# Cluster products and the sums and mean of w_out issued in halves, with a new order of work up to the first h

## The chip, the cores and the metric

The kernel runs on one core of a Trainium2 chip. One launch does the whole computation. The metric is the device time of that launch in microseconds (us); the median of three runs of the kernel before is 223.88 us, the lowest 223.83 and the highest 224.02. The profiles are of single executions, taken by the hardware profiler; each has a time of its own.

The core has engines that run beside each other, each with its own list of instructions that it works through in order: PE (the matrix engine; its weight loads are listed apart as PEld), DVE (VectorE), ACT (ScalarE), POOL (GpSimd) and SP (SyncE, which here only issues transfers). They wait for each other by semaphores.

## The reference

Two layers, cut to what matters. The first is attention in which a query sees only the keys of its own cluster:

```
q, k, v: (4, 8, 768, 64); centroids: (8, 16, 64)
q_assign = argmax(einsum('bhsd,hcd->bhsc', q_n, c_n))      # q_n, k_n, c_n: rows of length 1
k_assign = argmax(einsum('bhsd,hcd->bhsc', k_n, c_n))
mask     = q_assign[:, :, :, None] == k_assign[:, :, None, :]
scores   = where(mask, q @ k^T / sqrt(64), -1e9)
x        = softmax(scores) @ v                             # then laid out as (3072, 512)
```

The second works on each of the 3072 rows (tokens):

```
h    = x @ w_in                          # w_in (512, 1024)
solu = h * softmax(h)
ln   = (solu - mean(solu)) / sqrt(var(solu) + 1e-6) * g_ln
out  = ln @ w_out                        # w_out (1024, 512)
```

Since the mean that is taken from `solu` is the same number for all 1024 columns of a row, the kernel takes it out of `w_out` instead: it multiplies `w_out` by `g_ln`, subtracts from every row the mean over the 1024 rows, and multiplies `solu` by the result. For that it needs, once, the sums of `g_ln * w_out` over the rows, and their mean.

## The kernel before

The work is cut into named operations. A helper class, `Weave`, collects them (`add`, line 104) with the operations that each needs, and then issues them in an order that is written out by hand: `ORDER` (lines 28 to 78) has for each engine a list of kinds with counts ("S3" is the next three operations of kind S on that engine). What must wait for what on the chip comes from the data that the operations read and write, not from these lists; the lists only say what stands behind what on each engine.

The kinds that matter here:

- `ld`, `lv`, `li`, `lo` on SP: loads of q and k, of v, of w_in (four pieces `li0` to `li3`) and of w_out (four pieces `lo0` to `lo3`).
- `tp` on PE and `xa` on DVE or ACT (batch 0), `xt` on DVE (batches 1 to 3): q and k of a pair of heads transposed into a tile `xt`, one for q and one for k. `ca`: their cast into `qk`, from which the scores are made.
- `cl` on PE (`clusters`, line 445): the products of a pair's q and k with its centroids, into a tile `csc`. It is four float32 matmuls of 32 output rows and 384 columns, each in its own quarter (32 columns) of the PE array, two for q and two for k. The trace has two records for each float32 matmul.
- `tb`, `mx`, `oh`, `ot` on DVE: transpose, maximum, one-hot and transpose back (tile `oht`, in batch 0 a part of `w_out_c`); `pl`, mostly on POOL: the one-hots put under the rows of `qk`; `bl`: a part of them cleared. After that the scores of the pair can be made. One-hots on both sides add a constant to the scores of equal clusters, which serves as the mask.
- `S` on PE (`scores`): one bank of scores of 512 columns, mostly two matmuls of 256 columns; `E` on ACT (`expo`): its exponential; `V` on PE (`values`): the product with v for 128 queries, six matmuls. The scores have three banks (`ps_s`), so the bank of `S` number i is free when `E` number i-3 is done. `N` on DVE: division by the sums.
- `tx` on SP: x transposed by a transfer. `h` on PE (`f_h`): x times w_in for a block of 128 tokens, in four quarters of two matmuls each; `hm`, `ex`, `u`: maximum (DVE), exponential (ACT) and product (DVE); `tu`: u transposed by a transfer; `y` on PE (`f_y`): times w_out.
- `gs` on POOL, `su` on PE (`sum_w_out`, line 579), `sk` on DVE, `me` on PE (`mean_w_out`, line 592), `ce` on DVE: the mean taken out of w_out. `su0` and `su1` are four float32 matmuls each, of 32 output rows and 512 columns, again each in its own quarter of the PE array. `me` is one float32 matmul of 128 rows and 512 columns.
- `wi0` to `wi3` on POOL (line 561): the four quarters of w_in cast to bfloat16.

The four matmuls of one `cl`, in batch 0:

```python
for c in range(4):
    i, hh = divmod(c, 2)
    nc.tensor.matmul(csc[c * NB:(c + 1) * NB, :n], c_by_two[:, 2 * p + hh],
                     xts[b, p, i][:, hh * HALF:(hh + 1) * HALF],
                     tile_position=(0, c * NB))
```

Sixteen pairs of heads (four batches of four) go through `cl`, the first of them in two halves of the tokens. Batch 0 is worked off first in the order of the scores; the second layer begins, with the first `h`, about a fifth into the time, and from there scores, values, `h` and `y` of different blocks alternate on PE.

Of the kernel before, what the change touches and what calls it, by code (L numbers as in the profile page):

```python
# [10 lines left out]
F32 = mybir.dt.float32  # L11
# [11 lines left out]
class Weave:  # L23
# [3 lines left out]

    ORDER = {}
    ORDER["SP"] = """
        ld4 si ld4 lg lv ld2 lv ld3 lo ld lv ld2 lv ld2 lo2 ld3 lo ld4 li ld li3 tx ld lv  # L30
        ld3 lv tx ld3 tu ld8 lv tu tx ld lv ld4 tu ld3 ou ld2 ou ld tu ld12 tu ld4 lv ld2 ou
        tx ld3 tu ou ld2 tx lv ld tu ld4 tx ld tu ou2 ld lv ld4 tu ld4 tu ld ou ld7 pl ou ld
        lv2 ld3 tu lv tx ou tu lv pl ld4 ou2 tx lv tu tx ou tu pl2 tu2 tx tu tx ou2 tx ou tu
        tx2 ou tu2 ou2 tu2 ou6
    """
    ORDER["POOL"] = """
        po zo ca3 z ca pl ca bl pl2 ca bl ca pl sg cv z ca3 cv ca pl cv pl2 ca gs pl2 ca pl
        z ca2 cv2 z2 ca2 pl2 cv pl wi ca2 wi pl wi pl wi pl bl cv pl ca pl at pl cv al ca cv
        pl at ca bl pl cv ca3 al at ca al ca at ca pl2 bl cv pl2 ca4 at ca2 al ca pl2 bl pl2
# [5 lines left out]
        fl wm fl tp2 cp fl2 cl tp fl tp fl4 cl S3 tp2 S2 tp2 cq S2 tp S tp S2 tp S cl S2 V S  # L45
        tp S V S V S gt V S V2 S cl S V S V S V S tp S tp S2 tp S V S tp V2 S2 cl S3 V2 S V
        S V S2 V S V2 S2 V S cl S3 V2 S V S V S su S3 V2 S V S V S su S3 V2 S V2 S2 me S3 V2
        S V S V S cl S2 V S V S V2 S2 h S h S2 h2 S V2 S2 h V2 S h S V2 S2 h S V S V S h S h
        S2 V S h V S y2 V2 S2 y V S V S h3 S3 y V3 h V S2 V2 S cl S3 h2 S2 V3 S y2 S V h2 S
        V y2 S h S V h S2 h S y3 S2 y V3 h S3 cl V2 S V S y S2 y2 S3 V3 S y S2 V3 S2 cl S V  # L50
        S2 V2 S h S2 V2 S V S h S2 V2 cl V2 S3 y2 S V S2 V y S2 y V2 S3 h2 S V h S h S2 V h
        S V S V y2 S h V y2 S2 V S h3 S cl V S2 V2 S h V cl S3 h2 V y V S3 y2 V S h V3 S y S
        h S2 h2 S3 V2 y h S V S2 y V3 y S3 h3 y S3 V3 S h S V S V cl S V S h S cl V2 S3 y V2
        S y S2 y V2 S3 h y V S3 V h V2 S3 cl S2 V2 S y3 S2 y S V3 S V S y S2 V S V3 S2 y2 S3
        y V2 S2 h V2 S3 h3 S V S2 V y S V h2 V2 S y S2 y V y S h2 S3 cl h V S2 V3 S h V2 S3
        h2 S y S2 V h S2 V y2 V4 S3 y h S2 h V h V S V S y2 S3 V3 h2 S2 h2 S2 y2 S V S h2 S
        V3 S2 h S h S2 V S y V2 S V y2 S2 h2 S2 h2 V2 S2 V2 y S2 h V2 h V S2 h S V h S3 V2 h
        y S V y3 V h3 S2 y3 S2 y h2 V2 h y h y3 h V h V y4 h ptx h y4 h2 y3 h2 y ptu2 y6 ptu
        y ptu y5
    """  # L60
    ORDER["DVE"] = """
        cn xa cb ca tb mx oh ot pl2 tb mx oh ot xa3 cf xa2 ca cv tb xa mx oh gk N ot pl tb
        xa mx xa oh xa ot N tb mx pl N xt2 cv N oh ot N pl tb mx N oh ot sk xt N xt ce3 N ce
        tb ce ca ce2 N ce hm mx N u oh bn2 N hm ot ag xt u xt N bn2 hm ag sc xt u N bn tb hm
        mx bn oh ag u xt bn ot xt N cv hm bn ag sc xt tb mx N u xt oh ot sc N bn2 xt ag xt
        tb N hm mx tb N oh ot u xt mx N bn oh bn xt hm ot ag N cv u bn2 xt hm tb mx u N tb
        oh mx hm ot bn2 oh ag u N sc ag hm bn ot u bn N xt2 ag xt2 hm tb N bl mx tb bn2 oh u
        N xt ag xt sc hm ot tb mx oh N bn sc N u bn N ag xt ot bn ca N mx sc oh hm u bn ag N
        xt hm bn2 bl tb u ot ag N hm mx bn2 u bn N oh ot hm bl2 u ag N cv hm sc bn u N hm ag
        bn N bn u bn2 hm ag2 N bn u bn2 N ag hm bn u N ag hm bn2 u bn2 hm sc u N ag2 bn tx  # L70
        hm bn sc u bn ag hm bn tu ag u2 bn2 ag sc
# [104 lines left out]
def kernel(  # L176
# [185 lines left out]
    def apart(b, p):  # L362


        return by_token(b) and not halves_of(b, p)
# [76 lines left out]
            VEC[e].tensor_scalar(dst, src, scalar1=inv_C, scalar2=1.0,  # L442
                                 op0=Alu.mult, op1=Alu.mult)

    def clusters(b, p, hf):

        lo, n = (0, HALF) if hf is None else (hf * HALF, QTR)
        csc = ps_m.tile([P, HALF], F32, name="csc", tag="m")
        if apart(b, p):
            for c in range(4):  # L450
                i, hh = divmod(c, 2)
                nc.tensor.matmul(csc[c * NB:(c + 1) * NB, :n], c_by_two[:, 2 * p + hh],  # L452
                                 xts[b, p, i][:, hh * HALF:(hh + 1) * HALF],
                                 tile_position=(0, c * NB))
        for c in range(4) if not apart(b, p) else ():
            i, part = divmod(c, 2)
            nc.tensor.matmul(csc[c * NB:(c + 1) * NB, :n], c_bd[:, p, :],  # L457
                             xts[b, p, i][:, lo + part * n:lo + (part + 1) * n],
                             tile_position=(0, c * NB))
        asg[b, p, hf, "csc"] = csc  # L460
        asg[b, p, hf, "n"] = n

    def turn_back(b, p, hf):
        n = asg[b, p, hf, "n"]
# [111 lines left out]
    def spread_g():  # L576
        nc.gpsimd.tensor_copy(g_cols, g_ln2[:].unsqueeze(2).to_broadcast([P, n_fc, NB]))

    def sum_w_out(r):

        for c in range(4):
            fc = 4 * r + c
            uses(nc.tensor.matmul(hreg[c * NB:(c + 1) * NB, 1, :], g_cols[:, fc, :], w_g[:, fc, :],  # L583
                                  start=(r == 0), stop=(r == n_fc // 4 - 1),
                                  tile_position=(0, c * NB)), 1)
# [3 lines left out]
        uses(nc.scalar.copy(w_sum[:], src) if e == "ACT" else  # L589
             nc.vector.tensor_copy(w_sum[:], src), 1)  # L590

    def mean_w_out():
        uses(nc.tensor.matmul(hreg[:, 2, :], g_mean[:], w_sum[:]), 1, 2)  # L593

    def centre_w_out(fc):
        uses(nc.vector.scalar_tensor_tensor(out=w_out_c[:, fc, :], in0=w_g[:, fc, :],
# [393 lines left out]
    for idx, (b, p) in enumerate(pairs):  # L990
        first = first_of(b, p)
        for hf in range(2) if halves_of(b, p) else (None,):
# [6 lines left out]
            add(f"cl{t}", "PE", (0.72 - 0.22 * hf if half else 0.87), first - 9,  # L999
                (lambda e, b=b, p=p, hf=hf: clusters(b, p, hf)), kept + ["cf" if apart(b, p) else "cb"], take="m")  # L1000
# [116 lines left out]
    for f in range(n_f):  # L1117
# [113 lines left out]
    add("gs", "POOL", 0.35, 20, lambda e: spread_g(),  # L1231
        ["gk", "wm"] + [f"fl{j}" for j in range(n_idle)])
    for r in range(n_fc // 4):
        add(f"su{r}", "PE", 1.06, 30 + r, (lambda e, r=r: sum_w_out(r)),
            ["gs", f"lo{2 * r}", f"lo{2 * r + 1}"] + ring_free(1),
            last_tp[-1:] + [f"su{x}" for x in range(r)])
    add("sk", "DVE", 0.6, 34, keep_sums, [f"su{n_fc // 4 - 1}"], also={"ACT": 0.48})
    add("me", "PE", 0.9, 36, lambda e: mean_w_out(), ["sk", "sg"] + ring_free(2), last_tp[-1:])
    for fc in range(n_fc):
        add(f"ce{fc}", "DVE", 0.66, 44 + 0.5 * fc, (lambda e, fc=fc: centre_w_out(fc)),  # L1240
            ["me"] + [f"{x}0.{p}" for x in ("cl", "ot") for p in range(1, n_pair)],
            [f"ce{fc - 1}"] if fc else [])

    def clear(z):
# [35 lines left out]
```

## Time and profile before

| | |
|---|---|
| median of three runs | 223.88 us |
| the profiled execution, its time | 223.47 us |
| its span, first to last instruction | 221.6 us |
| PE busy | 215.8 us (97%) |
| DVE busy | 196.1 us (89%) |
| ACT busy | 191.8 us (87%) |
| POOL busy | 129.5 us (58%) |
| first `h` starts | 44.86 us |

The profiled execution's time is 1.87 us more than its span, and 0.41 us less than the median. A busy PE is not a PE at its peak: the ends of matmuls are modelled, and a matmul that waits in the array's queue counts as busy; so waits on PE are read from the distance between the starts of its pieces of work, not from its busy time. The granted clock of PE is 1.00 throughout, but for the last slice.

### The profile page before, as it was taken

Reading aid. Unit: us, or ns where it says so; the run is one execution under the profiler, and the core shown is the slowest. Engines: PE = TensorE matmul, PEld = TensorE weight load, DVE = VectorE, ACT = ScalarE, POOL = GpSimd, SP = SyncE. Lnnn points to the kernel's source line nnn. Section 1 sums busy time; section 2 is a strip of 40 time slices with the busy share of each in tenths; the row PEclk is TensorE's granted clock in tenths of the full one; section 3 lists DMA queues with packets and bytes.
Section 4 is the critical chain, followed back from the end, with each engine's and each line's share of the span. In section 5 each row is a group of like instructions: output and inputs, shape, how many; then the busy total and the mean of one; then the engine's idle time right before and its main releaser. Section 6 shows DMA issues by size and latency. Waiting matters only on the chain.

```text
span 221.6 us, 6609 instructions
## 1 busy us (share of the span) xinstructions
PE 215.8 (97%) x2420; PEld 147.5 (67%) x2420; DVE 196.1 (89%) x355; ACT 191.8 (87%) x372; POOL 129.5 (58%) x251
## 2 busy tenths in 40 slices
PE   7999999999999999999999999999999999999993
PEld 3667666766776687775677776777677677755452
DVE  4899987999999999999998989887999889888982
ACT  2799999999998999998899899999999998983362
POOL 3699891970886999538667724852895403022331
PEclk9999999999999999999999999999999999999998
DMA  6999999995798979999999998299831433666713
GB/s 144 364 283 264 269 180 289 255 213 103 123 251 149 226 129 166 222 205 171 180 209 175 180 204 181 77 219 191 236 59 26 82 69 123 96 137 171 182 71 131
DMA packets 125679, 38.80 MB, mean 175 GB/s; under 512 B 115016, under 2 KB 121168, under 8 KB 125648
## 3 DMA queue, kind: packets, MB, share of 16 engines
q1 hardware_dynamic: 123904, 37.87, 81.1%
q10 hardware_dynamic: 1744, 0.52, 1.0%
q8 instruction: 19, 0.31, 0.6%
q14 instruction: 12, 0.10, 0.2%
HBM read 23.11 MB, written 6.29 MB: 133 GB/s over the span
## 4 chain that ended last, share of the span: by engine, by line
PE 94%; ACT 1%; DVE 1%; issue 1%; DVEq 0%; ACTq 0%
PE sps L612 30%; PE hreg L723 19%; PE yps L787 18%; PE ops L637 15%; PE csc L457 5%; PE hreg L393 2%; PE idle_p L831 1%; ACT e L620 1%; PE csc L452 1%; PE hreg L583 1%; PE hreg L787 1%; PE utp L711 0%; PE hreg L593 0%; ACT e_sb L735 0%; DVE qk L523 0%
## 5 line engine op out<-in xcount | busy, mean ns | idle before, releaser
L620 ACT ACTIVATE e<-sps 128x512 bf16<-128x512 f32 (+1 forms) x288 | 148.6, 605 | 9.9 <-PE sps L612 8.6
L612 PE MATMUL sps<-qk 80*128 80x256 bf16 (+5 forms) x636 | 95.6, 264 | 0.8 <-ACT e L620 0.4
L612 PEld LDWEIGHTS <-qk 80*128 80x128 bf16 (+1 forms) x636 | 60.6, 121 | 26.7 <-issue 8.7
L637 PEld LDWEIGHTS <-e 128*128 128x128 bf16 x1134 | 49.9, 97 | 12.6 <-issue 1.9
L637 PE MATMUL ops<-v,e 128*128 128x65 bf16 x1134 | 55.0, 193 | 0.0
L723 PE MATMUL hreg<-w_in_sb,xT 128*128 128x512 bf16 x192 | 52.8, 379 | 0.0
L787 PE MATMUL yps<-w_out_c,uT 128*128 128x512 bf16 x184 | 48.9, 379 | 0.0
L523 POOL COPY qk<-oht 32x384 f32<-32x384 f32 (+1 forms) x48 | 23.7, 493 | 20.6 <-DVE oht L501 18.4
L742 DVE TENSOR_TENSOR u<-e_sb,hreg 128x1024 bf16<-128x1024 bf16 (+1 forms) x25 | 29.1, 1167 | 4.7 <-ACT e_sb L735 4.5
L753 DVE BATCH_NORM_STATS2 bs<-u 128x6 f32<-128x512 bf16 x48 | 31.4, 677 | 0.1
L729 DVE TENSOR_REDUCE nmax<-hreg 128x1 f32<-128x1024 f32 x24 | 29.0, 1209 | 2.5 <-PE hreg L723 2.2
L735 ACT ACTIVATE e_sb<-hreg,nmax 128x1024 bf16<-128x1024 f32 x24 | 26.9, 1122 | 4.6 <-DVE nmax L729 4.4
L442 POOL TENSOR_SCALAR qk<-xt 64x768 bf16<-64x768 f32 (+1 forms) x31 | 25.2, 813 | 2.0
L440 POOL CAST qk<-xt 64x768 bf16<-64x768 f32 (+1 forms) x30 | 24.2, 807 | 3.2 <-DVE xt L400 1.7
L787 PEld LDWEIGHTS <-uT 128*128 128x128 bf16 x200 | 18.2, 97 | 11.4 <-issue 0.3
L769 POOL TENSOR_SCALAR esq<-es,mv 128x1 f32<-128x1 f32 x24 | 8.5, 354 | 26.6 <-DVE mv L757 18.4
L723 PEld LDWEIGHTS <-xT 128*128 128x128 bf16 x192 | 16.9, 97 | 9.8 <-DVE u L742 0.6
L414 DVE STREAM_TRANSPOSE xt<-raw 128x768 f32<-128x768 f32 x24 | 22.6, 952 | 0.1
L662 DVE TENSOR_TENSOR x<-ops,den 128x256 bf16<-128x256 f32 (+1 forms) x39 | 18.9, 486 | 1.3
L763 POOL TENSOR_SCALAR es<-esum 128x1 f32<-128x1 f32 x24 | 5.3, 222 | 23.5 <-ACT e_sb L735 22.8
L541 POOL CAST v<-vf 128x384 bf16<-128x384 f32 x27 | 13.8, 527 | 1.8 <-DMA vf<-in_v_dram 0.9
L772 POOL TENSOR_TENSOR alpha<-esq,halves 128x1 f32<-128x1 f32 x24 | 13.5, 561 | 2.0
(84 smaller groups left out, 173.1 us busy)
## 6 DMA issues: line engine op xcount, KB each, us to landing
vf<-in_v_dram SPq DMA_DIRECT2D x16, 384.0 KB, 4.4
out_dram<-y SPq DMA_DIRECT2D x23, 256.0 KB, 2.5
raw<-in_q_dram SPq DMA_DIRECT2D x50, 96.0 KB, 3.9
raw<-in_k_dram SPq DMA_DIRECT2D x50, 96.0 KB, 2.8
w_g<-in_moe_w_out_dram SPq DMA_DIRECT2D x4, 512.0 KB, 6.7
w_st<-in_moe_w_in_dram SPq DMA_DIRECT2D x4, 512.0 KB, 6.9
raw<-in_q_dram SPq DMA_DIRECT2D x3, 384.0 KB, 5.5
raw<-in_k_dram SPq DMA_DIRECT2D x3, 384.0 KB, 6.0
```

Of the source, the lines that this page charges most:

```text
L440: VEC[e].tensor_copy(dst, src)
L442: VEC[e].tensor_scalar(dst, src, scalar1=inv_C, scalar2=1.0, op0=Alu.mult, op1=Alu.mult)
L523: ins = VEC[e].tensor_copy(dst.bitcast(F32), src.bitcast(F32).unsqueeze(1) .to_broadcast([NB, 2, n // 2]))
L612: nc.tensor.matmul(sps_[n, k][:, c0:c0 + w], side(b, h // 2, 1, h % 2, keys)[r], side(b, h // 2, 0, h % 2, slice(s0 * P, s0 * P + w))[r])
L620: nc.scalar.activation(es[n, k][:, :w], sps_[n, k][:, :w], Act.Exp, scale=exp_scale, bias=-exp_scale)
L637: nc.tensor.matmul(opss[g][:, s, :VW], es[n, k][:, c0:c0 + P], v1[slot(b, h // 2)][:, h % 2, kt, :VW], start=(kt == 0), stop=(kt == n_t - 1))
L723: uses(nc.tensor.matmul(hreg[:, at(f, f2)[1], :], xTs[f][:, dc, :], w_in_sb[:, dc, f2 * FF2:(f2 + 1) * FF2], start=(dc == 0), stop=(dc == ...
L729: uses(nc.vector.tensor_reduce(ff[f, "nmax"][:], pair_of(f), axis=AXY, op=Alu.max, negate=True), *both(f))
L735: uses(nc.scalar.activation(ff[f, "e"][:], pair_of(f), Act.Exp, bias=ff[f, "nmax"][:], accum_out=ff[f, "esum"][:]), *both(f))
L742: uses(nc.vector.tensor_tensor(ff[f, "u"][:, at_], ff[f, "e"][:, at_], pair_of(f)[:, at_], op=Alu.mult), *banks)
L753: nc.vector.bn_stats(ff[f, "bs"][:, f2, :], ff[f, "u"][:, f2, :])
L787: ins = nc.tensor.matmul(dst, ff[f, "uT"][:, at(f, f2)[0] * (n_fc // 2) + c, :], w_out_c[:, fc, cols], start=(fc == chunks[0]), stop=(fc = ...
```

## The change

Four things are changed; the computation is the same.

1. `clusters` takes a list of the four matmuls that it is to issue. For each of the 15 pairs after the first, `cl` becomes two operations: `cl{pair}.q` with the two matmuls of q and `cl{pair}` with the two of k. The first needs q's transposed tile only.
2. `su0` and `su1` become `su0.0`, `su0.1`, `su1.0` and `su1.1`, of two matmuls each. `me` becomes `me0` and `me1`, of 256 columns each.
3. The first quarter of the first `h` is listed as needing `wi0` and `wi1` only.
4. The lists for SP, POOL, PE and DVE are new up to about the first `h`; behind it they are the old ones, with "cl2" in the place of "cl" on PE. ACT's list is the same.

```diff
-    def clusters(b, p, hf):
+    def clusters(b, p, hf, of=range(4)):
...
-            for c in range(4):
+            for c in of:
                 i, hh = divmod(c, 2)
                 nc.tensor.matmul(csc[c * NB:(c + 1) * NB, :n], c_by_two[:, 2 * p + hh],
                                  xts[b, p, i][:, hh * HALF:(hh + 1) * HALF],
                                  tile_position=(0, c * NB))
...
-    def sum_w_out(r):
-
-        for c in range(4):
+    def sum_w_out(r, x):
+
+        for c in range(2 * x, 2 * x + 2):
             fc = 4 * r + c
             uses(nc.tensor.matmul(hreg[c * NB:(c + 1) * NB, 1, :], g_cols[:, fc, :], w_g[:, fc, :],
                                   start=(r == 0), stop=(r == n_fc // 4 - 1),
...
-    def mean_w_out():
-        uses(nc.tensor.matmul(hreg[:, 2, :], g_mean[:], w_sum[:]), 1, 2)
+    def mean_w_out(x):
+        cols = slice(x * d_model // 2, (x + 1) * d_model // 2)
+        uses(nc.tensor.matmul(hreg[:, 2, cols], g_mean[:], w_sum[:, cols]), 1, 2)
...
-                nd = [f"tx{fs[0]}"] + [f"wi{dc}" for dc in range(n_dc)]
+                nd = [f"tx{fs[0]}"] + [f"wi{dc}" for dc in range(n_dc if f or part else 2)]
```

Of PE's list, the line in which the sums stand in both:

```diff
-        S V S2 V S V2 S2 V S cl S3 V2 S V S V S su S3 V2 S V S V S su S3 V2 S V2 S2 me S3 V2
+        S V S V S su S2 V S V2 S V S cl S2 V S cl S V S2 V S su S2 V3 S2 V S su S2 su S2 V S
```

In the new order the two halves of a `cl` stand apart for five pairs, with scores (and here and there values) between them: pairs 1, 2 and 3 of batch 0 and pairs 0 and 1 of batch 1. For the other ten pairs the halves follow each other directly. The four pieces of `su` all stand apart from each other, and so do `me0` and `me1`.

The first place is the end of the sums on PE, `su1` (L583 in both; `hreg` is the PSUM region that takes the sums, `w_g` is w_out as loaded, `sps` a bank of scores, `ops` the values). Before:

```order
L637 MATMUL ops_828<-v1_2_107,e_812 128x65
L612 LDWEIGHTS qk3_102
L612 MATMUL sps_863<-qk3_102 128x256
L612 LDWEIGHTS qk3_102
L612 MATMUL sps_863<-qk3_102 128x256
L583 MATMUL hreg_111<-w_g_114,w_out_c_113 32x512 x4
```

Now, at the same place (the lines of the file have moved by one):

```order
L613 MATMUL sps_866<-qk3_102 128x256
L583 MATMUL hreg_111<-w_g_114,w_out_c_113 32x512 x2
L613 LDWEIGHTS qk3_102
L613 MATMUL sps_879<-qk3_102 128x256
L613 LDWEIGHTS qk3_102
L613 MATMUL sps_879<-qk3_102 128x256
L613 LDWEIGHTS qk3_102
L613 MATMUL sps_882<-qk3_102 128x256
L613 LDWEIGHTS qk3_102
L613 MATMUL sps_882<-qk3_102 128x256
L583 MATMUL hreg_111<-w_g_114,w_out_c_113 32x512 x2
```

Two banks of scores (`sps_879`, `sps_882`) have moved from behind the sum to between its two halves.

The second place is on PE too, the cluster products of pair 3 of batch 0 (`xt_505` is its q, `xt_546` its k). Before:

```order
L612 LDWEIGHTS qk1_100
L612 MATMUL sps_573<-qk1_100 128x256
L612 LDWEIGHTS qk1_100
L612 MATMUL sps_573<-qk1_100 128x256
L452 MATMUL csc_576<-xt_505,w_out_c_113 32x384 x2
L452 MATMUL csc_576<-xt_546,w_out_c_113 32x384 x2
L612 LDWEIGHTS qk1_100
```

Now:

```order
L613 MATMUL sps_572<-qk1_100 128x256
L454 MATMUL csc_575<-xt_505,w_out_c_113 32x384 x2
L613 LDWEIGHTS qk1_100
L613 MATMUL sps_582<-qk1_100 128x256
L613 LDWEIGHTS qk1_100
L613 MATMUL sps_582<-qk1_100 128x256
L454 MATMUL csc_575<-xt_557,w_out_c_113 32x384 x2
```

The bank of scores `sps_582` stood behind all four matmuls and now stands between those of q and those of k.

The third place is POOL around the casts of w_in (`w_in_sb<-w_st`, `wi0` to `wi3`); `qk_103<-xt` are casts of pair 0 of batch 1, `qk_103<-oht` its one-hots being put in place. Before:

```order
L513 COPY qk_102<-w_out_c 16x2x3x64
L561 CAST w_in_sb<-w_st 128x1024
L440 CAST qk_103<-xt 64x768 x2
L561 CAST w_in_sb<-w_st 128x1024
L523 COPY qk_103<-oht 32x2x192
L561 CAST w_in_sb<-w_st 128x1024
L523 COPY qk_103<-oht 32x2x192
L561 CAST w_in_sb<-w_st 128x1024
L523 COPY qk_103<-oht 32x2x192
L532 MEMSET qk_103 16x384
```

Now:

```order
L513 COPY qk_102<-w_out_c 16x2x3x64
L439 CAST qk_103<-xt 64x768
L523 COPY qk_103<-oht 32x2x192
L439 CAST qk_103<-xt 64x768
L523 COPY qk_103<-oht 32x2x192
L532 MEMSET qk_103 16x384
L561 CAST w_in_sb<-w_st 128x1024 x3
L523 COPY qk_103<-oht 32x2x192
L561 CAST w_in_sb<-w_st 128x1024
```

The first cast of w_in now stands behind two of the four copies that need the pair's one-hots, which come from DVE; before, it stood ahead of them.

More of the change, by code (lines that the diff above doesn't have):

```diff
@@ L60 @@
+        y S V3 S V S y S2 V S V3 S2 y2 S3 y V2 S2 h V2 S3 h3 S V S2 V y S V h2 V2 S y S2 y V
+        y S h2 S3 cl2 h V S2 V3 S h V2 S3 h2 S y S2 V h S2 V y2 V4 S3 y h S2 h V h V S V S
+        y2 S3 V3 h2 S2 h2 S2 y2 S V S h2 S V3 S2 h S h S2 V S y V2 S V y2 S2 h2 S2 h2 V2 S2
+        V2 y S2 h V2 h V S2 h S V h S3 V2 h y S V y3 V h3 S2 y3 S2 y h2 V2 h y h y3 h V h V
+        y4 h ptx h y4 h2 y3 h2 y ptu2 y6 ptu y ptu y5
     """
@@ L443, in cast @@
                                  op0=Alu.mult, op1=Alu.mult)
-    def clusters(b, p, hf):
+    def clusters(b, p, hf, of=range(4)):
         lo, n = (0, HALF) if hf is None else (hf * HALF, QTR)
-        csc = ps_m.tile([P, HALF], F32, name="csc", tag="m")
+        if 0 in of:
+            asg[b, p, hf, "csc"] = ps_m.tile([P, HALF], F32, name="csc", tag="m")
+            asg[b, p, hf, "n"] = n
+        csc = asg[b, p, hf, "csc"]
         if apart(b, p):
-            for c in range(4):
+            for c in of:
                 i, hh = divmod(c, 2)
@@ L454, in clusters @@
                                  tile_position=(0, c * NB))
-        for c in range(4) if not apart(b, p) else ():
+        for c in of if not apart(b, p) else ():
             i, part = divmod(c, 2)
@@ L459, in clusters @@
                              tile_position=(0, c * NB))
-        asg[b, p, hf, "csc"] = csc
-        asg[b, p, hf, "n"] = n
     def turn_back(b, p, hf):
@@ L998 @@
             old = last[-3] if len(last) >= 3 else None
-            add(f"cl{t}", "PE", (0.72 - 0.22 * hf if half else 0.87), first - 9,
-                (lambda e, b=b, p=p, hf=hf: clusters(b, p, hf)), kept + ["cf" if apart(b, p) else "cb"], take="m")
+            by = ["cf" if apart(b, p) else "cb"]
+            if half:
+                add(f"cl{t}", "PE", 0.72 - 0.22 * hf, first - 9,
+                    (lambda e, b=b, p=p, hf=hf: clusters(b, p, hf)), kept + by, take="m")
+            else:
+                add(f"cl{t}.q", "PE", 0.435, first - 9,
+                    (lambda e, b=b, p=p: clusters(b, p, None, range(2))),
+                    kept[:len(kept) // 2] + by, take="m")
+                add(f"cl{t}", "PE", 0.435, first - 8.9,
+                    (lambda e, b=b, p=p: clusters(b, p, None, range(2, 4))),
+                    kept[len(kept) // 2:] + by, [f"cl{t}.q"])
             add(f"tb{t}", "DVE", 0.37 if half else 0.56, first - 20,
@@ L1232 @@
         ["gk", "wm"] + [f"fl{j}" for j in range(n_idle)])
+    sums = [f"su{r}.{x}" for r in range(n_fc // 4) for x in range(2)]
     for r in range(n_fc // 4):
[L1234 to L1238, printed above, removed]
+        for x in range(2):
+            add(f"su{r}.{x}", "PE", 0.53, 30 + r + 0.5 * x, (lambda e, r=r, x=x: sum_w_out(r, x)),
+                ["gs", f"lo{2 * r + x}"] + ring_free(1),
+                last_tp[-1:] + sums[:2 * r + x])
+    add("sk", "DVE", 0.6, 34, keep_sums, sums[-1:], also={"ACT": 0.48})
+    for x in range(2):
+        add(f"me{x}", "PE", 0.45, 36 + 0.5 * x, (lambda e, x=x: mean_w_out(x)),
+            ["sk", "sg"] + ring_free(2), last_tp[-1:] + ["me0"] * x)
     for fc in range(n_fc):
         add(f"ce{fc}", "DVE", 0.66, 44 + 0.5 * fc, (lambda e, fc=fc: centre_w_out(fc)),
-            ["me"] + [f"{x}0.{p}" for x in ("cl", "ot") for p in range(1, n_pair)],
+            ["me1"] + [f"{x}0.{p}" for x in ("cl", "ot") for p in range(1, n_pair)],
             [f"ce{fc - 1}"] if fc else [])
```

57 lines of the change are left out of this document (26 added, 31 removed).

## The prediction

> **What bounds the kernel now.** First the page's head, then the busy times by stretch, cut where the first `h` starts (44.8) and where the second layer is in full swing (52).
>
> ```profile
> span 221.6 us, 6609 instructions
> ...
> PE 215.8 (97%) x2420; PEld 147.5 (67%) x2420; DVE 196.1 (89%) x355; ACT 191.8 (87%) x372; POOL 129.5 (58%) x251
> ```
> ```profile
> core 0: us, PE busy (x) PEld busy (x) DVE busy (x) ACT busy (x) POOL busy (x), PEclk, DMA share, GB/s
> 9.00:20.00 11.00, 11.00 (x125) 7.80 (x125) 10.35 (x23) 10.62 (x28) 9.28 (x18) 1.00 1.06 296
> 20.10:44.80 24.70, 24.45 (x330) 16.81 (x329) 21.62 (x43) 23.35 (x48) 18.04 (x30) 1.00 1.08 249
> 44.80:52.00 7.20, 6.92 (x73) 4.63 (x72) 6.69 (x12) 6.98 (x15) 3.56 (x6) 1.00 0.82 159
> 52.00:215.00 163.00, 162.94 (x1830) 112.24 (x1829) 150.19 (x255) 144.92 (x276) 92.63 (x178) 1.00 0.80 156
> ```
>
> From 52 to 215 PE is idle for 0.06 us of 163, while ACT has 18 us to spare. The order there is as it was. So a microsecond that PE loses or gains before 52 arrives at the end whole: the change is worth the work that it adds to PE, less the waits that it takes from PE, before 52.
>
> In the stretch 20.1 to 44.8 PE and ACT are close to each other. How much of PE's time there is waiting is read from its work, by line, from 20.1 to the start of a bank of scores at 51.9:
>
> ```profile
> L612 PE MATMUL sps<-qk 80*128 80x256 bf16 x114 | 19.4, 272 | 0.5 <-ACT e L620 0.4
> L637 PE MATMUL ops<-v,e 128*128 128x65 bf16 x222 | 10.8, 193 | 0.0
> L723 PE MATMUL hreg<-w_in_sb,xT 128*128 128x512 bf16 x14 | 4.0, 379 | 0.0
> L583 PE MATMUL hreg<-w_g,w_out_c 128*32 128x512 f32 x16 | 2.1, 604 | 0.0
> L457 PE MATMUL csc<-xt,c_bd 128*32 128x384 f32 x16 | 1.7, 498 | 0.0
> L393 PE MATMUL hreg<-ident_f,raw 128*128 128x128 f32 x8 | 1.4, 272 | 0.0
> L593 PE MATMUL hreg<-w_sum,g_mean 128*128 128x512 f32 x2 | 1.0, 592 | 0.0
> L452 PE MATMUL csc<-xt,w_out_c 128*32 128x384 f32 x8 | 0.9, 498 | 0.0
> ```
>
> Those durations overlap and hold waits. What a piece costs the queue is its distance to the next start, which the chain of waits gives (start, us, what):
>
> ```profile
> 21.78 0.33 PE hreg L393 x3
> 22.11 0.36 PE ops L637 x12
> 22.47 0.44 PE sps L612 x4
> 22.91 0.78 PE csc L452 x8
> ...
> 28.28 0.29 PE sps L612 x2
> 28.57 0.78 PE csc L457 x8
> ...
> 31.48 0.31 PE sps L612 x2
> 31.78 0.99 PE hreg L583 x8
> ...
> 34.43 0.38 PE sps L612 x2
> ...
> 38.63 0.86 PE hreg L593 x2
> ...
> 45.02 0.43 PE hreg L723 x2
> ```
>
> A score matmul costs 0.11, a value 0.03, a quarter of `h` 0.43, three transposes 0.33, `cl` 0.78, `su` 0.99, `me` 0.86. The counts by these prices: 12.5 + 6.7 + 3.0 + 0.9 + 3 x 0.78 + 2 x 0.99 + 0.86 = 28.3 of 31.8 us. Of the other 3.5, two scores just ahead of a `cl` or `su` take 0.29 to 0.31 where 0.22 would do: 0.09 for each of five entries, 0.45. The rest, 3.0, is scores and values that wait for ACT (34.43: 0.38 for two). Some 0.7 of it lies behind the first `h`: in the order of time,
>
> ```profile
> 49.97 0.54 PE L637 MATMUL ops<-v,e 128*128 128x65 bf16 x12
> 50.68 0.86 PE L612 MATMUL sps<-qk 80*128 80x256 bf16 x4 [0.17 <-ACT e L620]
> 51.45 0.61 PE L723 MATMUL hreg<-w_in_sb,xT 128*128 128x512 bf16 x2
> ```
>
> the next start comes 0.71 after twelve values that cost 0.36, and 0.77 after four scores that cost 0.44. So 2.3 us of PE's waits lie between 20.1 and 44.8.
>
> **The halves: do they cost half?** This decides the case. The four matmuls of a `cl` run at the same time, in four quarters of the array: 16 records of 498 ns are 8.0 us and cover 1.7. Two records belong to a matmul, one behind the other. `me` shows what one matmul costs alone: 0.86 for 512 columns, so 0.65 for 384 (384/512). `su`, four at once with 512 columns, costs 0.99, only 0.13 more than one. Two at once must lie between one and four: 0.65 to 0.78 for half a `cl`, 0.86 to 0.99 for half a `su`. The 0.09 at the entry shows that changing from full-width to quarter-width work costs something; a like cost on the way out would be most of the 0.13, and a pair pays it as four do. So I take values nearer the upper rows, 0.75 and 0.95. The scores between two halves use the whole width, so nothing fills the two quarters that stand empty.
>
> The Trainium skill ("TensorE: Matmul & The Clock Gate", Part 3, "Measured speedup vs the span model") has a rule for matmuls packed beside each other: the span is one matmul's duration and about 4 ns for each further one. By it half a `cl` would cost 8 ns less than the whole, and the sum below would be about 0.35 us higher; the 0.99 against 0.86 is near this. The same section has a measured speedup of 2.38 for three quarters, which would make three cost 1.26 of one; that is the milder case taken up under the rivals.
>
> - `cl`: apart for five pairs. Each costs 2 x 0.75 - 0.78 = 0.72, and a second entry of 0.09 (bounded by 0 and 0.09, the row being the only one): 0.81, five times 4.05. Bounds for a pair at 0.65 and 0.78: 0.61 and 0.87, so 3.0 and 4.35.
> - `cl` of the other ten pairs: the halves follow each other directly, the same four matmuls stand next to each other, 0.
> - `su`: two, each 2 x 0.95 - 0.99 + 0.09 = 1.0, so 2.0. Bounds with 0.86 and 0.99: 1.6 and 2.2.
> - `me`: the same columns in two pieces, one more entry at most twice 0.09: 0 to 0.2, taken as 0.1.
>
> Added to PE: 6.15 us, from 4.6 to 6.75.
>
> **The waits that go.** ACT's side of the stretch 20.1 to 44.8, exponentials alone:
>
> ```profile
> 20.10:44.80 24.70, 22.98 (x47) 1.00 1.08 249
> ```
>
> 47 exponentials, 0.49 each. PE's work in the stretch is 24.7 - 2.3 = 22.4 now and becomes 22.4 + 3 x 0.81 + 2.0 + 0.1 = 26.9 (three of the five split products lie in it), against ACT's 23.0. The pieces stand in the new order at distances of one to five banks; a bank with its share of values costs PE 0.22 + 0.12, so over five banks PE gains 0.7 us on ACT and then loses 0.75 to 0.95 at the next half. It hardly gets far enough ahead to wait: ACT now waits for PE. I let 2.0 of the 2.3 go. The 0.7 behind the first `h` stays: the scores at 50.68 wait for an exponential that stands on ACT behind the first block's `ex`, and the new order has the same work between the block's last quarter and these scores (five banks, six sets of values, two quarters: 3.5 us) as the old. Bounds: nothing goes, or all 3.0.
>
> **Other moves.** SP issues `lo3` ahead of the loads of pair 1 of batch 1 and the loads of v later; DVE has `tb`, `xt` and a cast in other places; `gs` is one place later on POOL. I cost these at nothing, hidden behind a PE that comes later by up to 4 us at each point; if one were later than that, PE would wait for it by the difference. The one that I checked closely is the third place:
>
> ```profile
> 36.17 0.58 DVE L501 STREAM_TRANSPOSE oht<-oh 128x384 bf16<-128x384 bf16 x1
> ```
> ```profile
> 38.34 1.04 POOL L561 CAST w_in_sb<-w_st 128x1024 bf16<-128x1024 f32 x1 [4.88 <-PE sps L612]
> 39.33 1.70 POOL L440 CAST qk<-xt 64x768 bf16<-64x768 f32 x2
> ...
> 42.20 0.50 POOL L523 COPY qk<-oht 32x384 f32<-32x384 f32 x1
> ```
> ```profile
> 44.86 0.59 PE L723 MATMUL hreg<-w_in_sb,xT 128*128 128x512 bf16 x2
> ```
>
> The casts of w_in now stand behind the one-hots of pair (1,0). These come from the `cl` of that pair and, on DVE, from behind an `N` that waits for values on PE. Both come later by four split products and a split `su` (4.2) less the waits gone by then (some 1.5): 36.2 + 2.7, and a cast that DVE now does ahead of them (0.85, as one takes on POOL): 39.75, done 0.58 later at 40.3. POOL then has a copy of 0.5, a cast of 0.85, a copy, the clearing (taken as a copy), three casts of w_in, a copy and the fourth cast: 0.85 + 4 x 0.5 + 4 x 1.04 = 7.0, until 47.3. PE is at the first `h` at 44.86, plus 0.44 for two banks of scores that now stand ahead of it, plus 4.2: 49.5. That leaves 2 us in hand. `x`'s transposes likewise move with PE.
>
> **The sum.** 6.15 - 2.0 = +4.15 us, on the profiled execution's 223.47: 227.6. That execution was 0.41 below the median of 223.88, so against the median it is 228.0. From both ends: 4.6 - 3.0 = +1.6, and 6.75 - 0 = +6.75.
>
> **The rivals.**
>
> 1. *Half costs half* (the other side). If a pair took half of what four take, only the second entries would be added, 7 x 0.09 + 0.1 = 0.7; and PE's waits could go until ACT bounds the stretch, 24.7 - 23.0 = 1.7. Then 222.9. For it: better-spread pieces do feed ACT. Against: two records in a row per matmul, and one alone at 0.86. It decides from the point at which a pair of a `cl` costs under 0.48 (then the added work equals 2.0). Chance 0.06.
> 2. *A pair costs what one does* (0.65 and 0.86). Added 4.6, less 2.0: +2.6, 226.5. For it: fewer at once cannot be slower. The skill's 2.38 points this way: with 0.13 for each further matmul a pair is 0.81 of four, which would give an estimate of +2.3. Chance 0.13.
> 3. *The first `h` waits for POOL.* If DVE gives the one-hots more than 2 us later than reckoned, each further microsecond is PE's; at 4 us late 230. For it: POOL already waited 4.88 ahead of the first cast. Chance 0.07.
> 4. *The ten undivided pairs are no longer taken together* because each half waits for itself: 10 x 0.72, 235.2. Against: q and k had different producers before, too, and the four ran together. Chance 0.03.
>
> My forecast has 0.70, with its own range 227.1 to 229.3 (half a `cl` at 0.72 to 0.78 and half a `su` in proportion, waits gone 2.5 to 1.2); 0.01 is left for no change. The range 225.5 to 230.6 is the two ends of the sum; rivals 1 and 4 lie outside it. A difference under 0.2% (0.45 us) can't be told from none: faster 0.05, same 0.02, slower 0.93.
>
> **What would show it.** In the profile after: a `cl` of four records and not eight in the chain, at about 0.75; `su` of four at about 0.95; 0.44 of scores between them. PE's waits for ACT in the stretch before the first `h` nearly gone, and ACT's idle time there up by some 3 us, waiting for scores. The first `h` later by about 4.6, and the distance from it to the end as before. The forecast is wrong if a split `cl` shows near 0.4, if the first `h` waits for `w_in_sb`, or if PE is idle behind 60.

## The result and the profile after

| | before | after |
|---|---|---|
| median | 223.86 us (4 runs, 223.62 to 224.02) | 227.54 us (4 runs, 227.49 to 228.02) |
| ratio | | 1.0167, 95% interval 1.0151 to 1.0182 |
| span of the profiled execution | 221.6 us | 225.6 us |
| first scores start | 8.92 us | 9.33 us |
| first `h` starts | 44.86 us | 49.81 us |

The kernel became slower, by 3.7 us. In the ratios, and in the medians given for the experiments below, executions that took over 1.5% longer than the fastest of the same kernel are left out. From here on the lines of the file have moved by one (in the experiments by a few more): exponentials are L621, scores L613, values L638, `cl` L459 (L454 in batch 0), `su` L583, `me` L594, `h` L724.

The page's head after:

```profile
span 225.6 us, 6574 instructions
...
PE 218.4 (97%) x2390; PEld 147.9 (66%) x2422; DVE 196.9 (87%) x355; ACT 192.5 (85%) x372; POOL 129.0 (57%) x251
```

The program has as many matmuls as weight loads, 2422, two more than before for the second piece of `me`; 32 matmul records are missing in this trace. With them missing, PE's busy time rose by 2.6 us only for a span that is 4.0 longer; in the second profile of this kernel (after_again, below), which has all 2422, it is 220.4, 4.6 more than before.

The stretches that answer to those of before, cut at the same pieces of work:

```profile
core 0: us, PE busy (x) PEld busy (x) DVE busy (x) ACT busy (x) POOL busy (x), PEclk, DMA share, GB/s
22.10:49.70 27.60, 27.60 (x335) 17.05 (x333) 23.48 (x44) 24.71 (x49) 20.62 (x33) 1.00 0.81 200
49.70:57.00 7.30, 6.98 (x83) 4.96 (x82) 6.23 (x11) 6.53 (x14) 1.16 (x3) 1.00 0.67 166
57.00:219.00 162.00, 160.18 (x1783) 111.31 (x1811) 149.29 (x255) 144.08 (x275) 90.95 (x175) 1.00 0.81 157
```

and in the first of them the exponentials alone:

```profile
22.10:49.70 27.60, 24.39 (x48) 1.00 0.81 200
```

The exponentials now leave 3.2 us of 27.6 free, where they left 1.7 of 24.7. ACT waits for PE. (The idle 1.8 us of PE in the last stretch go with the missing records: the shift against before does not grow there, below.)

PE's work in that stretch, by line:

```profile
L613 PE MATMUL sps<-qk 80*128 80x256 bf16 x97 | 16.7, 273 | 0.0
L638 PE MATMUL ops<-v,e 128*128 128x65 bf16 x186 | 9.4, 193 | 0.0
L583 PE MATMUL hreg<-w_g,w_out_c 128*32 128x512 f32 x16 | 4.2, 605 | 0.0
L459 PE MATMUL csc<-xt,c_bd 128*32 128x384 f32 x16 | 3.4, 498 | 0.0
L454 PE MATMUL csc<-xt,w_out_c 128*32 128x384 f32 x8 | 1.7, 498 | 0.0
L392 PE MATMUL hreg<-ident_f,raw 128*128 128x128 f32 x8 | 1.4, 276 | 0.0
L594 PE MATMUL hreg<-w_sum,g_mean 128*128 128x256 f32 x4 | 1.2, 379 | 0.0
```

The same 16, 16 and 8 records of `su` and `cl`, each as long as before (605 and 498 ns), now cover 4.2, 3.4 and 1.7 us where they covered 2.1, 1.7 and 0.9. That is the change in one view: two at a time instead of four, twice as long in all.

What the pieces cost the queue, from the chain of waits (start, us, what):

```profile
24.82 0.77 PE csc L454 x4
25.59 0.33 PE sps L613 x2
25.91 0.77 PE csc L454 x4
...
31.54 0.77 PE csc L459 x4
...
38.47 0.98 PE hreg L583 x4
39.46 0.54 PE sps L613 x4
40.00 0.98 PE hreg L583 x4
...
42.92 0.43 PE hreg L594 x2
...
49.98 0.43 PE hreg L724 x2
```

Half a `cl` costs 0.77, a whole one 0.78. Half a `su` costs 0.98, a whole one 0.99. Two scores behind a half take 0.33 and four 0.54, which is 0.11 and 0.10 over the price. By these prices the stretch is full: 97 scores x 0.11 + 186 values x 0.03 + 4 x 0.98 + 6 x 0.77 + 8 transposes x 0.11 + 0.86 for `me` is 26.5; ten entries of 0.09 and another 0.1 behind the first half of `me` make 27.5 of 27.6. Next to no wait is left in it.

The second step of the prediction, that undivided pairs of halves still run together, is one row of the chain, later (all four matmuls, 0.78 as before):

```profile
67.91 0.78 PE csc L459 x8
```

**Where the 4 us come from.** The first `h` starts 4.95 later, of which 0.44 is two banks of scores that now stand ahead of it: 4.51. The starts of nearly all later `hm`, `ex` and divisions are 4.4 later than before, 4.3 towards the end, and the span is 4.0 longer: little is won or lost behind the first `h`, and the last 0.3 us, behind the last of these, were not followed further. The 4.51 are made of

- the start: the first scores stand at 9.33 instead of 8.92, 0.41;
- five `cl`, each 2 x 0.77 - 0.785 + 0.09 = 0.845: 4.2;
- two `su`, each 2 x 0.985 - 1.0 + 0.09 = 1.06: 2.1; `me` 0.1;
- less 2.3, all of the waits that PE had between 20 and 45.

### The profile page after: what moved, and what is told of

The parts are those of the page before. It is cut to its first block, busy times and chain, and to the rows that moved or that the text cites. A ratio compares the mean times of both kernels' runs of the same rounds, so it can differ in the third digit from the quotient of the medians.

```text
span 225.6 us, 6574 instructions
## 1 busy us (share of the span) xinstructions
PE 218.4 (97%) x2390; PEld 147.9 (66%) x2422; DVE 196.9 (87%) x355; ACT 192.5 (85%) x372; POOL 129.0 (57%) x251
## 4 chain that ended last, share of the span: by engine, by line
PE 88%; ACT 2%; issue 2%; DVE 2%; DMA 1%; SPq 1%; POOL 0%; ACTq 0%; DVEq 0%
PE sps L613 28%; PE hreg L724 16%; PE yps L788 16%; PE ops L638 14%; PE csc L459 5%; PE hreg L392 2%; PE csc L454 2%; ACT e L621 2%; PE hreg L583 2%; DMA raw<-in_q_dram 1%; PE idle_p L832 1%; PE hreg L788 1%; DVE u L743 1%; SPq L405 0%; PE utp L712 0%
## 5 line engine op out<-in xcount | busy, mean ns | idle before, releaser
L621 ACT ACTIVATE e<-sps 128x512 bf16<-128x512 f32 (+1 forms) x288 | 149.2, 601 | 13.0 <-PE sps L613 11.0
L613 PE MATMUL sps<-qk 80*128 80x256 bf16 (+5 forms) x636 | 95.1, 264 | 0.6 <-DVE qk L523 0.3
L613 PEld LDWEIGHTS <-qk 80*128 80x128 bf16 (+1 forms) x636 | 59.4, 121 | 28.9 <-issue 10.4
L638 PEld LDWEIGHTS <-e 128*128 128x128 bf16 x1134 | 50.1, 97 | 12.7 <-issue 1.9
L638 PE MATMUL ops<-v,e 128*128 128x65 bf16 x1134 | 54.9, 193 | 0.1
L724 PE MATMUL hreg<-w_in_sb,xT 128*128 128x512 bf16 x174 | 49.2, 379 | 1.0
L788 PE MATMUL yps<-w_out_c,uT 128*128 128x512 bf16 x170 | 46.5, 379 | 0.6
L441 POOL TENSOR_SCALAR qk<-xt 64x768 bf16<-64x768 f32 (+1 forms) x31 | 24.6, 795 | 2.4 <-ACT xt L399 0.5
L724 PEld LDWEIGHTS <-xT 128*128 128x128 bf16 x192 | 16.8, 97 | 9.8 <-issue 0.6
```

The lines of the kernel that those rows point to most:

```text
L441: VEC[e].tensor_scalar(dst, src, scalar1=inv_C, scalar2=1.0, op0=Alu.mult, op1=Alu.mult)
L613: nc.tensor.matmul(sps_[n, k][:, c0:c0 + w], side(b, h // 2, 1, h % 2, keys)[r], side(b, h // 2, 0, h % 2, slice(s0 * P, s0 * P + w))[r])
L621: nc.scalar.activation(es[n, k][:, :w], sps_[n, k][:, :w], Act.Exp, scale=exp_scale, bias=-exp_scale)
L638: nc.tensor.matmul(opss[g][:, s, :VW], es[n, k][:, c0:c0 + P], v1[slot(b, h // 2)][:, h % 2, kt, :VW], start=(kt == 0), stop=(kt == n_t - 1))
L724: uses(nc.tensor.matmul(hreg[:, at(f, f2)[1], :], xTs[f][:, dc, :], w_in_sb[:, dc, f2 * FF2:(f2 + 1) * FF2], start=(dc == 0), stop=(dc == ...
L788: ins = nc.tensor.matmul(dst, ff[f, "uT"][:, at(f, f2)[0] * (n_fc // 2) + c, :], w_out_c[:, fc, cols], start=(fc == chunks[0]), stop=(fc = ...
```

## The experiments

The theory: a pair of matmuls in two quarters of the array costs PE what four in four quarters cost, so each division that has scores between its halves adds a second full price; the waits that are saved pay for a third of it. Its rivals: the new order of the other engines costs something by itself, or the price is particular to this stretch. All ratios are against runs of the kernel before on the same chip.

**joined**: the new order, with the halves of the five `cl`, of `su` and of `me` behind each other, at the place of the second half. (The lines with a minus are PE's list of the changed kernel. In the section on the change that line has `cl S V S2`, where the kernel has `cl S V2 S2`.)

```diff
...
-  S V S V S su S2 V S V2 S V S cl S2 V S cl S V2 S2 V S su S2 V3 S2 V S su S2 su
+  S V S V S3 V S V2 S V S3 V S cl2 S V2 S2 V S su2 S2 V3 S2 V S3 su2
...
```

> The changed kernel with the two halves of each divided cl, su and me issued directly one behind the other again, at the place of the second half; all lists else as in the changed kernel. Theory (each half that stands apart costs PE nearly a whole burst): the 6.4 us of added PE work goes (5 x 0.845 + 2 x 1.07 + 0.1), and at most the 2.3 us of waits come back: 221.2 to 223.9 us. Rival (the new order of the other work costs the time, not the halving): 226 to 227.5 us.

Measured: 225.07 us (10 runs, 224.16 to 227.04), ratio 1.0045 (1.0014 to 1.0075). So the halves standing apart are the larger part of the loss, some 2.5 of 3.7 us. But the time is not that of before, and lies above what was expected. The chain of waits of this run, at and behind a `cl` that is whole again:

```profile
24.71 0.78 PE csc L455 x8
...
29.74 0.69 ACT e L622
...
30.48 0.38 PE sps L614 x2
...
31.35 0.78 PE csc L460 x8
```

Between 25.9 and 30.4 the chain runs through ACT's exponentials. PE waits again, 2.9 us in all between 20 and 45 by the distances of its pieces, against 2.3 in the kernel before: the new order was laid out for pieces that stand apart. Ahead of 20 it waits some 0.6 us more than before, too; there the chain runs through ACT until 13.8:

```profile
12.63 1.16 ACT e L622 x3
13.79 0.04 issue
13.83 0.32 PE sps L614
```

The first scores stood at 9.48, 0.56 later than before. The first `h` starts at 47.25, 2.39 later than before, of which 0.44 is again the two banks of scores; the start and these waits cover the rest within some 0.2. In the profiled execution, whose time of 226.65 is above the median, PE fell back by another 1.65 us between 94 and 106, which stands in no term of the prediction. The larger part is a wait for a transfer of x ahead of an `h`, the smaller one for a transfer of u ahead of a `y`; in the order of time,

```profile
98.56 1.04 PE L725 MATMUL hreg<-w_in_sb,xT 128*128 128x512 bf16 x4 [0.95 <-DMA xT<-x]
...
103.19 1.04 PE L789 MATMUL yps<-w_out_c,uT 128*128 128x512 bf16 x4 [0.23 <-DMA uT<-u]
```

and in the chain:

```profile
97.82 5.33 DMA uT<-u
```

What made x late was not followed. The transfer that turns u round took 5.33 us behind loads of v and k that SP's new list puts there (SP's list is new up to its ninth `tu`, and not only up to about the first `h`); the median of these transfers in the kernel before is 3.6. In the changed kernel PE comes 4 us later to this place, and its shift stays level there.

**other_lists**: the new lists of SP, POOL and DVE, and PE's list of before, with the halves as neighbours.

```diff
...
-  S V S V S su S2 V S V2 S V S cl S2 V S cl S V2 S2 V S su S2 V3 S2 V S su S2 su
+  S2 V S V2 S2 V S cl2 S3 V2 S V S V S su2 S3 V2 S V S V S su2 S3
...
```

> The changed kernel with PE's list of before (halves directly behind each other); SP, POOL and DVE by the new lists. Theory (the other engines' order is covered by PE): 223.9 us, within 0.5. Rival (the new order of SP, POOL or DVE costs part of the 3.7 us): 225 us or more.

Measured: 223.96 us (10 runs, 223.22 to 225.34), ratio 0.9999 (0.9974 to 1.0024). The new lists of the other engines, and the division of the code as such, cost nothing that can be measured, which here means less than some 0.6 us. The loss is made by PE's list.

**sums_joined** and **products_joined**: the changed kernel with only `su` joined, and with only `cl` joined. For the first

```diff
...
-  S V S V S su S2 V S V2 S V S cl S2 V S cl S V2 S2 V S su S2 V3 S2 V S su S2 su
+  S V S V S3 V S V2 S V S cl S2 V S cl S V2 S2 V S su2 S2 V3 S2 V S3 su2
...
```

and for the second

```diff
...
-  S V S V S su S2 V S V2 S V S cl S2 V S cl S V2 S2 V S su S2 V3 S2 V S su S2 su
+  S V S V S su S2 V S V2 S V S3 V S cl2 S V2 S2 V S su S2 V3 S2 V S su S2 su
...
```

> The changed kernel with only the halves of su0 and su1 directly behind each other again, at the place of the second; cl still apart. Theory (each half that stands apart costs PE nearly a whole burst): 2 x (2 x 0.985 - 1.0 + 0.09) = 2.1 us less on PE, of which at most 0.5 comes back as waits: 225.4 to 226.0 us. Rival (su's halving is not what costs): 227 to 227.6 us.

> The changed kernel with only the halves of the five divided cl directly behind each other again, at the place of the second; su still apart. Theory: 5 x 0.845 = 4.2 us less on PE, of which up to 1.5 comes back as waits: 223.3 to 224.9 us; this and the run with su joined together give back more than the run with both joined, since the waits come back only once. Rival (the order is what costs): 226.5 us or more.

Measured: 226.54 us (4 runs, 226.49 to 227.75), ratio 1.0101 (1.0037 to 1.0166), and 225.52 us (10 runs, 225.01 to 225.96), ratio 1.0043 (1.0010 to 1.0076). Both saved less than expected, since more waits came back. Whole sums save 2.1 us of work and gave 1.0; in the profile 1.1 us of waits are back. Whole products save 4.2 and gave 2.0; in the profile some 2.3 of waits are back, 0.8 of them ahead of 20, as in joined. The chain of waits of products_joined shows such a stretch of ACT behind a half of `su`, here the last one before `me`:

```profile
38.50 0.98 PE hreg L584 x4
...
44.22 0.70 ACT e L622
...
44.96 0.38 PE sps L614 x2
```

So a term of the sum cannot be taken out alone: in these orders, in which PE is loaded just past ACT, about half of what was taken from PE came back as waits (in joined 3.7 of 6.4).

**sums_apart**: the lists of before on all engines, and only the halves of the two sums apart.

```diff
...
-  S2 V S V2 S2 V S cl2 S3 V2 S V S V S su2 S3 V2 S V S V S su2 S3 V2 S V2 S2 me2
+  S2 V S V2 S2 V S cl2 S3 V2 S V S V S su S3 su V2 S V S V S su S2 su S V2 S V2 S2 me2
...
```

> The kernel before with its own lists and only the two halves of each sum (su0, su1) set apart by two or three banks of scores; all cluster products whole. Theory (each half that stands apart costs PE nearly a whole burst, less the waits that it fills): +2.1 us on PE, and of the 1.0 us of waits between 28 and 45 us 0.3 to 0.9 go: 225.1 to 225.7 us. Rival (a half costs half): 223.0 to 223.9 us. Rival (a pair costs what one matmul does): 224.6 to 225.0 us.

Measured: 225.40 us (5 runs, 225.27 to 225.68), ratio 1.0064 (1.0042 to 1.0085), as expected. The price shows in the order of before just as in the new one:

```profile
32.23 0.98 PE hreg L587 x4
33.21 0.76 PE sps L617 x6
33.97 0.98 PE hreg L587 x4
```

**late_apart**: the lists of before, the early products whole, and the halves of the ten late `cl` set apart by one bank of scores. Nothing else is changed, and PE is the bound there.

```diff
...
-  S3 y V3 h V S2 V2 S cl2 S3 h2 S2 V3 S y2
+  S3 y V3 h V S2 V2 S cl S2 cl S h2 S2 V3 S y2
...
```

> The price of a half by itself: all lists of before, the early halves directly behind each other, but the halves of the ten late cluster products (pairs 2 and 3 of batch 1, all of batches 2 and 3) stand one bank of scores apart, where PE has no waits to give. Theory: each costs 2 x 0.77 - 0.785 and a second entry of 0.09, 0.845, ten times: +8.45, 232.3 us (231.8 to 232.8). Rival (a pair costs what one matmul does, 0.65): +6.0, 229.9 us. Rival (half costs half): +0.9, 224.8 us.

Measured: 234.19 us (4 runs, 233.75 to 234.63), ratio 1.0440 (1.0396 to 1.0484). The chain of waits:

```profile
63.69 0.77 PE csc L464 x4
64.46 0.57 PE sps L618 x4
65.03 0.77 PE csc L464 x4
```

Ten times 0.845 is 8.45 of the 10.4 us by which the span grew; 0.2 is a later start (first scores at 9.10). The rest was not expected: a product ends 1.3 us later (its second price and four scores), and DVE stands waiting for it. DVE's waits and PE's, of this run:

```profile
DVE cst L471 <- PE csc L464: 10.4, 9, 2.1
...
PE yps L793 <- DVE cst L471: 1.0, 3, 0.3
```

and DVE's of the kernel before:

```profile
DVE cst L466 <- PE csc L457: 0.9, 3, 0.3
```

DVE, which was busy for 89% of the span in the kernel before, waits 10.4 us (nine times) for the products instead of 0.9, and PE in turn 1.0 for a `y` that is let go by DVE's transpose of a product. The last 0.8 us are not assigned to a wait. This is also the fourth rival of the prediction made real: ten late products whose halves do not run together cost 10 us.

**by_columns**: can a product be divided without the double price? Here each half keeps all four matmuls and takes half of the columns, 192 of `cl` and 256 of `su` (the first halves of both sums come ahead of the second halves); the lists are those of the change.

```diff
-    def clusters(b, p, hf, of=range(4)):
+    def clusters(b, p, hf, x=None):
...
+        m0, m1 = (0, n) if x is None else (x * n // 2, (x + 1) * n // 2)
...
-            for c in of:
+            for c in range(4):
...
-                nc.tensor.matmul(csc[c * NB:(c + 1) * NB, :n], c_by_two[:, 2 * p + hh],
-                                 xts[b, p, i][:, hh * HALF:(hh + 1) * HALF],
+                nc.tensor.matmul(csc[c * NB:(c + 1) * NB, m0:m1], c_by_two[:, 2 * p + hh],
+                                 xts[b, p, i][:, hh * HALF + m0:hh * HALF + m1],
```

> The changed kernel with its lists, but each half of cl and su has all four matmuls on half of the columns (192 and 256) in place of two matmuls on all; the sums of su are then done for the first half of the columns first. Theory (the price hangs on how many quarters of the array run at once): a half costs about half, and with 0.1 to 0.2 for each second entry and its end seven of these add 0.7 to 1.4 us, against waits of up to 2.3 us: 222.0 to 224.0 us. Rival (any second burst costs a fixed 0.8 to 1 us, or the order is at fault): 227 us or more.

Measured: 223.83 us (8 runs, 223.07 to 224.69), ratio 0.9988 (0.9963 to 1.0012). With the lists of the change and a cheaper half, no loss is left that can be measured: it was the double price. The chain of waits:

```profile
22.55 5.92 DMA w_g<-in_moe_w_out_dram
...
28.52 0.63 PE hreg L585 x4
...
31.08 0.46 PE csc L460 x8
```

Half a `cl` costs 0.46, more than half of 0.785, and with the second entry a division adds 0.23 instead of 0.845. A half of `su` costs 0.57, and adds 0.23 as well. The first of them, which now needs both first pieces of w_out, waited 1.6 us for the second of these to land. That wait and a late start (first scores at 9.37) are more than the 1.1 us by which the span of this execution, 222.7, is still above that of before.

**columns_su_later** and **before_columns**: two attempts to keep the gain of the halves by columns. The first is by_columns with the first sum behind the `cl` of pair (1,0) and SP's list of before; the second has the lists of before, in which only the `cl` of three pairs and the sums are divided by columns and stand apart.

```diff
...
-  S3 cl S cl S2 V2 S V S V S su S2 V S V2 S V S cl S2 V S cl S V2 S2 V S su S2 V3 S2 V S su S2 su
+  S3 cl S cl S2 V2 S V S V S3 V S V2 S V S cl S2 V S cl S su V2 S2 V S2 su S V3 S2 V S su S2 su
...
```
```diff
...
-  S V S2 V S V2 S2 V S cl S3 V2 S V S V S su S3 V2 S V S V S su S3 V2 S V2 S2 me
+  S V S2 V S V2 S2 V S cl S2 cl S V2 S V S V S su S3 V2 S su V S V S su S3 su V2 S V2 S2 me
...
```

> As the run by columns (all four matmuls in each half, on half of the columns), with the first sum moved behind the cluster products of pair 0 of batch 1, so that it does not wait for the second load of w_out, and SP's list of before. Theory: halves by columns add 5 x (2 x 0.465 - 0.785 + 0.09) + 2 x (2 x 0.57 - 1.0 + 0.09) + 0.1 = 1.7 us to PE, and the 2.3 us of waits go; the 1.8 us that the first sum waited in the run by columns goes too: 223.0 to 223.8 us. Rival (it was no wait for a load, or the new order costs by itself): 224.5 us or more.

> The kernel before with its own lists, in which only three cluster products (pair 3 of batch 0, pairs 0 and 1 of batch 1) and the two sums are halved by columns and set apart by a few banks. Theory: it adds 3 x 0.235 + 2 x 0.23 = 1.2 us to PE and takes 1.2 to 1.8 us of waits: 223.2 to 223.9 us. Rival (every second burst costs a whole one): 227 us or more.

Measured: 223.96 us (9 runs, 223.49 to 226.30), ratio 1.0009 (0.9970 to 1.0049), and 224.52 us (10 runs, 223.48 to 226.02), ratio 1.0020 (0.9986 to 1.0055). Neither came out faster, and both lie above what was expected. In before_columns five divisions by columns add 1.17 us, and about 1.0 of PE's waits are gone: its first `h` starts at 45.06, before at 44.86. The 47 exponentials of the stretch take 22.98 of 24.7 us, so, as long as they take that time, the most that an order of PE can win there is 1.7 us less what the division costs. No version here is faster than the kernel before by more than can be measured.

**after_again** and **before_again**: both kernels once more, for the 0.4 us at the start.

> The changed kernel once more, on the same chip as the run beside it: 227.5 us (227.0 to 228.1). First scores at 9.3 to 9.5 us if the lists set it, at any of 8.9 to 9.5 if it is chance.

> The kernel before once more, for its profile: in the profiles so far PE's first scores began at 8.9 to 9.1 us in the four kernels with PE's old list and at 9.3 to 9.5 in the six with the new one, with the same work ahead of them. If the lists are the cause, 8.9 to 9.1 here; if it is chance from one execution to the next, either.

Measured: after_again 227.13 us (4 runs, 227.00 to 227.50), ratio 1.0135 (1.0104 to 1.0166), first scores at 9.29; before_again 223.65 us in one run, first scores at 9.05. The first `h` comes 4.77 us later in this pair (49.77 and 45.00), 4.33 without the two banks; without the start, 0.24 here and 0.41 above, both pairs leave 4.1. The loss is confirmed, with 3.0 to 3.7 us in the two comparisons; the start is taken up in the last section.

## Why the prediction was right

The time was forecast as 228.0 and came out as 227.54, in the forecast's own range of 227.1 to 229.3, by the mechanism that was forecast.

- *PE is the bound, and what is lost before 52 arrives at the end.* Right. The shift was 4.4 behind the first `h` and 4.0 in the span.
- *A pair pays nearly what four do.* Right, and this decided the case. The prediction took 0.75 and 0.95, from between one matmul (0.65 and 0.86) and four (0.78 and 0.99); measured were 0.77 and 0.98, at the upper rows. Its reason, a cost of changing between full and quarter width that a pair pays as four do, fits the halves by columns (last section). The Trainium skill ("TensorE: Matmul & The Clock Gate", Part 3, "Measured speedup vs the span model") has the rule by which the pair would cost 8 ns less than four; this trace has about 15 ns less, so it is near that step of the rule, and not near the 2.38 of the same section, which would have made a pair 0.81 of four. Its first step does not fit: one matmul of 512 columns, `me`, costs 0.86 here, and a pair 0.98; but `me` has the full width, and one quarter alone was not run. Had the upper rows been taken, the term would have been 6.4 instead of 6.15, as the accounting above gives it. (Two small slips in the sums: the lower end of 4.6 has the full second entry in it and would be 4.1 without; and the estimate for rival 2 from the 2.38 comes to +2.4, not +2.3.)
- *A second entry costs 0.09.* Right: 0.09 to 0.11 behind each half.
- *2.0 of 2.3 us of waits go.* Low by 0.3: all of them went. ACT's idle time rose by 1.5 in the stretch, and not by the 3 that were given as a sign. The stretch is 2.9 longer; it holds one exponential more (0.5), and the exponentials show 0.508 each (24.39 over 48) instead of 0.489. Their records last 0.61 in both and overlap when they follow each other closely; an ACT that waits between them shows more busy time for the same work, which fits the other 0.9.
- *The undivided pairs run together.* Right, 0.78 for eight records; late_apart shows what it would have cost otherwise.
- *POOL's casts of w_in are in time.* Right, to a tenth: the one-hots were reckoned done at 40.3, and the last cast at 47.3. POOL in order of time:

```profile
40.17 0.50 POOL L523 COPY qk<-oht 32x384 f32<-32x384 f32 x1 [3.08 <-DVE oht L501]
...
46.27 1.04 POOL L561 CAST w_in_sb<-w_st 128x1024 bf16<-128x1024 f32 x1
```

  The first `h` started at 49.81, with 2.5 us in hand.
- *The other moves cost nothing.* Right by other_lists, ratio 0.9999. One risk was not seen: in joined PE waits between 97 and 103 for SP's transfers of x and u, where the changed kernel, 4 us later there, does not.
- *The start.* Not in the sum: in the profiled executions it added 0.41. The pair's price (0.25 low), the start (0.41), the waits (0.3 too few) and what the end gave back (0.5) nearly cancel: 4.0 in the span, for 4.15 forecast. That it came so near is luck; that two divided quarters cost as much as four, and that PE passes this on to the end, is not. Against the medians it is 3.7, since the profiled execution of before was 0.41 below its median and that of after was not.

What the prediction did not work out was how the terms hang together. Added work and waits gone were two sums with a minus between them; sums_joined and products_joined show that about half of what is taken from PE here comes back as waits.

## What to carry to other kernels

In this kernel, float32 matmuls that fill quarters of the array side by side are paid as a group: two quarters cost what four do, so such a group should be issued whole or, if it must be divided, by columns with all quarters in each part. Before work is spread to fill waits, set the price of its second entry and second group against the waits that are there, and against the point at which the next engine bounds the stretch. And read waits of a matrix engine from the distances between starts: a doubling of the cover with the same records and the same duration of each is the sign that things no longer run beside each other.

## What the runs showed of the hardware

- *A group has a fixed part.* Half of the columns cost 0.46 of 0.785 for `cl`, and 0.57 of 1.0 for `su`: about 0.14 us per group that does not shrink with the columns, beside the 0.09 at its entry. It belongs to the visit and not to the matmuls: in by_columns the ten late pairs have their halves directly behind each other, and both together cost 0.79:

```profile
65.04 0.79 PE csc L460 x16
```

  With `me` as the price of one matmul (0.86 for 512 columns, so 0.65, 0.43 and 0.32 for 384, 256 and 192), each of these groups costs one matmul of its columns and 0.12 to 0.15 us, with two quarters as with four. So a division by quarters pays that matmul a second time, and one by columns only the fixed part and the entry.
- *The start differs by 0.4 us between executions.* The first transposes on PE, in the chain of before, of after and of sums_apart:

```profile
4.34 1.23 PE hreg L393 x6
...
8.92 0.65 PE sps L612 x3
```
```profile
4.34 0.64 PE hreg L392 x3
...
5.10 0.88 PE hreg L392 x3
...
9.33 0.65 PE sps L613 x3
```
```profile
4.34 1.28 PE hreg L396 x6
...
9.37 0.65 PE sps L617 x3
```

  Such a transpose takes 0.21 us until PE has its full clock and 0.11 after it. Full clock is taken from where the trace's record of the granted clock begins, at 1.00 (in the kernel before at 5.18, so that the "throughout" given for it holds from there on). It came 4.9 to 5.5 us into the span in five executions, with the first scores at 8.92 to 9.10, and 5.9 to 7.2 us in eight, with the first scores at 9.29 to 9.48. All executions with the new list of PE were among the eight; but sums_apart, which has the old list up to there, was too, so the list is not the cause. The cause was not found.
- *A transfer can show late.* Between 94 and 108 PE lost 1.65 us in joined, most of it for a transfer of x and the rest for one of u, and 0.3 to 0.55 in other_lists and products_joined (u) and in columns_su_later (x). The last of these has SP's list of before, so that the smaller losses are not shown to come from SP's order. The changed kernel lost nothing there.
